# Loading chunk 4's queries after the second half of the values, behind a hold on chunk 2's third unit, in a fused sorted-attention and gated-MLP kernel

## The chip, the cores and the metric

The kernel runs on one core of one Trainium2 chip. The metric is the device time of one execution in microseconds (us), lower is better. The engines named below are TensorE (PE, matrix products and transposes by the identity), VectorE (DVE), ScalarE (ACT), GpSimd (POOL), and SyncE (SP), which here only issues DMAs. The DMAs of a core run on 16 DMA engines. Those that POOL issues stand in one queue (q0 in the profile, "software dynamic"), those that SP issues in another (q1, "hardware dynamic").

## What is computed

Two stages follow each other: attention over keys and values whose blocks are mixed by a normalized 8 x 8 matrix for each head, then a gated MLP with the cosine as gate. B = 4, H = 8, S = 768, D = 64, 8 blocks of 96 rows, 3072 tokens, model width 512, inner width 2048; inputs and output are float32.

```python
for _ in range(5):                       # P: (B, H, 8, 8), from sort_net
    P = exp(P - P.max(-1)); P /= P.sum(-1) + 1e-9; P /= P.sum(-2) + 1e-9
k_sorted = einsum('bhij,bhjcd->bhicd', P, k_blocks)
v_sorted = einsum('bhij,bhjcd->bhicd', P, v_blocks)
scores = q_blocks @ k_sorted_blocks.T / sqrt(D)      # 96 x 96 per block
attn = softmax(scores)
x = (attn @ v_sorted_blocks) -> (3072, 512)
h = x @ w_in
out = (h * cos(h)) @ w_out
```

## The kernel before

The 3072 tokens are worked on as eight chunks of 384 tokens, numbered 0 to 7: chunk n is one half (four blocks) of batch n // 2, for all 8 heads. A unit (n, u) is block u of chunk n, with its 8 heads. Batches 0 and 1 (chunks 0 to 3) are group 0, batches 2 and 3 (chunks 4 to 7) are group 1; keys and values of group 1 are loaded and sorted while chunks 1 to 3 are worked on.

The whole program is an order written out by hand (lines 845 to 1173): nothing reorders it, each engine runs its instructions in the order of the calls, and waits by semaphores where data or a buffer is not ready. The calls that matter here are:

- `qk(n, u)` (line 491; `qk_half` for one half): PE forms the scores of a unit (L438), DVE takes the row maximum (L487) and subtracts it (L489). `q_of(n, ...)` reads `q_turned[n % 2]`, so chunks 2, 4 and 6 share the tile `q_turned[0]`, and 3, 5 and 7 the tile `q_turned[1]`.
- `expo(n, u)` (line 510): ACT takes the exponential into one of three buffers `p_buf` (L515). With `on_pe` false SP then issues a DMA transpose of it into a tile called `pT` (L533), which is "the turn" of the unit; otherwise PE turns it later (`p_transpose`, L550).
- `av(n, u)` (line 555): PE multiplies the turned exponentials by the sorted values (L570), DVE divides by the sum (L581, L583). PE can't begin before the unit's turn has landed. Its PSUM tile comes from the pool `big`, which has three buffers that the scores, the key products (`k_sort_g`, L408, evicted by ACT) and others take in turn.
- `up`, `down`: the two products of the MLP (L614, L639); ACT takes the cosine (L618), DVE the gate (L622), and SP stores the result (L629).
- `load_q(n)` (line 115): from chunk 3 on, eight DMAs on POOL's queue (L129), one for each block and each parity of the head, which read 96 x 4 runs of 64 float32 numbers and write them as bf16. Chunks 4 and 6 go to the tile `q_mem`, chunks 3, 5 and 7 to a part of `kv` (the name of the tile that also holds the values).
- `q_transpose_dma(n)` (line 147): two DMA transposes on SP's queue (L149) which turn the loaded queries into `q_turned[n % 2]`. Each needs its half of the eight loads.
- `load_pair(vbuf, vin_d, lo, hi)` (line 90): one sixth of the values of group 1 on POOL's queue (L92). `v_permute` (line 169) are copies on POOL (L179) that put them into `vperm` in the order in which `v_sort_g` (L458) reads them.
- `p_hold(n, u)` (line 543): POOL copies one column of the unit's turn into a scrap tile `held` (L541). It computes nothing: it makes POOL wait until that turn has landed, and all that POOL issues later with it.
- `k_swap(kT2)` (line 420): two DMAs on SP's queue (L421, L422) that complete the sorted keys of group 1, which the scores of chunk 4 need.

POOL issues DMAs in eight lanes that are used in turn (semaphores DMASW0 to DMASW7): an issue waits until the DMA eight before it, on the same lane, has landed. SP's DMAs do the same with the lanes DMAHW0 to DMAHW7.

On POOL the stretch around the change stands in this order: `zeros_between(3)`, `load_q(3)`, a hold on keys, the first half of the values (three DMAs), `zeros_between(4)` (two memsets of `q_mem`, L137), `load_q(4)`, the hold on unit (2, 2), the second half of the values (three DMAs), `v_permute`, a memset, the hold on unit (3, 3), `load_q(5)`. On SP it is: `q_transpose_dma(3)`; the turns of units (2, 0), (2, 1), (2, 2); two stores; the turn of (3, 0); a store; `q_transpose_dma(4)`; `k_swap(kT2)`; the turns of (3, 1) and (3, 2). On PE, after the eight `up` of chunk 1 and scores of chunk 2, stand: parts of `down(1, ...)` with key products between, `av(2, 0)`, `qk(3, 0)`, key products, half of a `down`, key products, `av(2, 1)`, and so on.

Of the kernel before, what the change touches and what calls it, by code (L numbers as in the profile page):

```python
# [18 lines left out]
def kernel(  # L19
# [70 lines left out]
    def load_pair(buf, src, lo, hi):  # L90

        nc.gpsimd.dma_start(  # L92
            out=buf[:, lo:hi], in_=src[2:4].rearrange("b r x -> (b r) x")[:, lo:hi])
# [11 lines left out]
    def q_zeroed(n):  # L105

        return kbuf[:blk, :2 * (QZ + D)] if n % 2 else q_mem[:]
# [7 lines left out]
    def load_q(n):  # L115
        b, ih = n // 2, n % 2
        if n < NQ:

            nc.gpsimd.dma_start(
                out=q_rows, in_=q[b][:, ih * IC * blk:(ih + 1) * IC * blk].rearrange(  # L120
                    "h (p r) d -> p h (r d)", r=QR))
        else:
            src = q[b].rearrange("h (i c) d -> c i h d", c=blk).rearrange(
                "c i (h e) d -> c i h e d", e=2)
            q_heads = q_zeroed(n).rearrange("p (e x) -> p e x", e=2)[:, :, :QZ].rearrange(
                "p e (i h w) -> p i h e w", i=IC, h=H2)[:, :, :, :, :D]
            for i in range(IC):
                for e in range(2):
                    nc.gpsimd.dma_start(  # L129
                        out=q_heads[:, i, :, e], in_=src[:, ih * IC + i, :, e])  # L130
# [38 lines left out]
    def v_permute(rows, lo=0, halves=True, step=VQ, hi=D):  # L169

        for z in range(lo, hi, step):
            dst = vperm[rows, :CD].rearrange("p (d c) -> p d c", d=D)[:, z:z + step]
            src = vv[rows, z:z + step, :blk]
            if halves:
                dst = dst.rearrange("p d (x t) -> p d x t", x=2)
                src = src.rearrange("p d (t x) -> p d x t", x=2)
            nc.gpsimd.tensor_copy(dst, src)  # L179
# [231 lines left out]
    def k_sort_g(t0, eng, pool, tag):  # L411
        ps = pool.tile([128, 4, 4 * NB], FP32, name="ks", tag=tag)
        for t in range(4):
            k_products(ps, t, t0 + t, slice(0, 128), bds[1].rearrange("p x i -> p (x i)"),
                       pair)
        copy_on(
            eng, kT2[:, ::2, :, :, t0:t0 + 4].rearrange("p e b m t -> p b e m t"),
            ps.rearrange("p t (b e m) -> p b e m t", b=2, e=2))
# [91 lines left out]
    def expo(n, u, on_pe=False):  # L510
        p = p_bufs[cnt[0] % NP]
        cnt[0] += 1


        nc.scalar.activation(  # L515
            p[:, :, :blk], s_t.pop((n, u)).rearrange("p e h c -> p (e h) c"), AF.Exp,
            scale=scale)
        if u == 0 and n in (NQ, NQ + 1):

            w = 2 * H2 * blk  # L520
            c = 2 * (QZ + D) + (n - NQ) * w
            t = kbuf[:, c:c + w].rearrange("p (a c) -> p a c", c=blk)
        elif n < LATE:
            t = ptp.tile([128, 2 * H2, blk], BF16, name="pT", tag="pT")
        else:

            z, w = (n * IC + u) % 8, 2 * H2 * blk
            t = vperm[:, z * w:(z + 1) * w].rearrange("p (a c) -> p a c", c=blk)
        pT[n, u] = t
        if on_pe:  # L530
            pb[n, u] = p
        else:
            nc.sync.dma_start_transpose(out=t[:], in_=p.rearrange("p a c -> p (a c)"))  # L533
# [9 lines left out]
    def p_hold(n, u):  # L543
        hold(pT[n, u])
# [542 lines left out]
    expo(2, 3, True)  # L1087
    down(1, 1, 1, nc.sync)
    k_sort_g(12, A, *B)
    load_q(4)  # L1090
    p_hold(2, 2)
    for z in range(3, 6):
        load_pair(vbuf, vin_d, z * CD // 6, (z + 1) * CD // 6)
    expo(3, 0)
    v_permute(slice(0, 128))
    av(2, 1, True)
# [106 lines left out]
```

## Time and profile before

| | |
|---|---|
| Median of three runs | 239.36 us (236.26, 239.67, 239.36) |
| The profiled execution's own time | 238.81 us |
| Its span (first to last instruction) | 236.9 us |
| Outside of the span | 1.9 us |
| PE busy | 224.1 us, 95% of the span |
| DVE, ACT, POOL busy | 170.9, 154.6, 95.9 us |
| Mean granted PE clock over the span | 0.993 |
| DMA moved | 31.19 MB in 67672 packets |

All times within the span are counted from its start. A row of the timeline gives the start, the duration, the engine, the line, the operation, what it writes and reads, how many instructions are merged in it, and in brackets how long the engine sat idle before it and which instruction ended that. In the view by stretches "PEclk" is the clock that PE was granted, 1.00 being full, and "DMA share" is the summed busy time of packets over that of 16 engines. It can exceed 1, since the time of a packet counts from when it is begun, also while another is in work beside it.

### The profile page before, as it was taken

What the parts mean: (1) busy time and instruction counts of PE and PEld (TensorE: products, weight loads), DVE (VectorE), ACT (ScalarE), POOL (GpSimd) and SP (SyncE); (2) the same over time, 40 slices, a digit from 0 to 9 for tenths busy, and PEclk for the clock granted to TensorE, in tenths of its full rate; (3) what the DMA queues carried; (4) which work ended last, traced back from release to release, by engine and by line L of the source; (5) the groups of instructions that cost most, each with busy time, mean ns of one, the idle gap of its engine ahead of it and who ended that gap; (6) DMA issues with size and microseconds to landing.
All of it is one profiled execution on the core that took longest, in us unless ns stands there. A gap on an engine that the chain in (4) does not pass through costs nothing.

```text
span 236.9 us, 5401 instructions
## 1 busy us (share of the span) xinstructions
PE 224.1 (95%) x2191; PEld 142.1 (60%) x2212; DVE 170.9 (72%) x291; ACT 154.6 (65%) x209; POOL 95.9 (40%) x121
## 2 busy tenths in 40 slices
PE   8678999999999699999999999999999999999994
PEld 3367898567665366655666555655665566455554
DVE  6769867969699546895568985898599759835700
ACT  4648877777889347886788845673767466826611
POOL 8999998399992209900807100900000000000000
PEclk9999999999999799999999999999999999999999
DMA  7999999993999996659999778964942470251012
GB/s 91 209 196 205 204 221 217 201 237 100 112 151 157 175 190 128 68 133 162 106 155 115 79 92 148 220 67 92 165 161 38 81 199 0 50 157 46 3 44 89
DMA packets 67672, 31.19 MB, mean 132 GB/s; under 512 B 56384, under 2 KB 63168, under 8 KB 67392
## 3 DMA queue, kind: packets, MB, share of 16 engines
q0 software_dynamic: 24048, 13.64, 42.0%
q1 hardware_dynamic: 43312, 17.02, 34.7%
q8 instruction: 17, 0.28, 0.5%
q10 hardware_dynamic: 288, 0.20, 0.3%
q14 instruction: 7, 0.06, 0.1%
HBM read 27.27 MB, written 6.29 MB: 142 GB/s over the span
## 4 chain that ended last, share of the span: by engine, by line
PE 78%; DMA 10%; DVE 3%; POOL 3%; ACT 3%; issue 2%; SPq 0%; ACTq 0%; DVEq 0%; POOLq 0%
PE h L614 30%; PE o L639 24%; DMA kv<-in_v_dram 5%; PE h L798 5%; PE o L819 4%; DMA pT<-p_buf 4%; PE sc L438 4%; PE av L570 3%; POOL vperm L179 2%; PE o L1167 1%; DMA kTs<-kTs 1%; PE ks L408 1%; DVE xn L583 1%; PE vs L458 1%; ACT p_buf L515 1%
## 5 line engine op out<-in xcount | busy, mean ns | idle before, releaser
L614 PE MATMUL h<-xT,w_in_t 128*128 128x384 bf16 x448 | 78.4, 326 | 0.0
L639 PE MATMUL o<-w_out_t,gg 128*128 128x512 bf16 x305 | 75.2, 383 | 1.0 <-issue 0.2
L622 DVE TENSOR_TENSOR gg<-c,h 128x768 bf16<-128x768 f32 x56 | 52.7, 949 | 19.6 <-ACT c L618 19.6
L618 ACT ACTIVATE c<-h,half_pi 128x768 f32<-128x768 f32 x56 | 50.5, 901 | 24.6 <-PE h L614 23.6
L614 PEld LDWEIGHTS <-w_in_t 128*128 128x128 bf16 x448 | 42.2, 98 | 26.3 <-DVE xT L259 0.3
L639 PEld LDWEIGHTS <-gg 128*128 128x128 bf16 x320 | 29.5, 100 | 28.9 <-issue 1.7
L179 POOL COPY vperm<-kv 64x768 bf16<-64x768 bf16 (+2 forms) x12 | 28.3, 2398 | 10.2 <-PE xps L601 5.6
L515 ACT ACTIVATE p_buf<-s 96x768 bf16<-96x768 f32 x32 | 26.7, 843 | 5.5 <-DVE s L489 4.7
L489 DVE TENSOR_TENSOR s<-sc,mx 96x384 f32<-96x384 f32 (+1 forms) x33 | 24.3, 736 | 1.6
L487 DVE TENSOR_REDUCE mx<-sc 96x4 f32<-96x384 f32 (+1 forms) x33 | 24.0, 728 | 0.0
L583 DVE TENSOR_TENSOR xn<-av,r 96x512 bf16<-96x512 f32 x32 | 22.0, 686 | 1.1
L581 DVE RECIPROCAL r<-av 96x8 f32<-96x8 f32 x32 | 6.4, 199 | 15.2 <-PE av L570 15.0
L257 ACT CAST kTs<-ks 128x512 bf16<-128x512 f32 x20 | 11.3, 582 | 8.5 <-PE ks L408 7.5
L129 POOL DMA_DIRECT2D kv<-in_q_dram x24 | 16.0, 681 | 0.8 <-DMA xT<-xn 0.3
L438 PE MATMUL sc<-kTs,q_turned 128*128 128x96 bf16 x224 | 15.6, 207 | 0.4 <-DMA kTs<-kTs 0.4
L438 PEld LDWEIGHTS <-q_turned 128*128 128x128 bf16 x224 | 12.6, 98 | 4.1 <-DVE s L489 0.6
L257 ACT COPY kv<-o 128x512 f32<-128x512 f32 (+2 forms) x10 | 5.2, 524 | 14.1 <-PE o L639 11.5
L819 PE MATMUL o<-w_out_t,gg 128*128 128x512 bf16 x45 | 11.2, 379 | 0.2
L798 PE MATMUL h<-xT,w_in_t 128*128 128x192 bf16 x128 | 11.1, 246 | 0.0
L259 DVE COPY kv<-o 128x512 f32<-128x512 f32 (+1 forms) x5 | 3.1, 612 | 11.1 <-PE o L1167 8.5
L129 POOL DMA_DIRECT2D q_mem<-in_q_dram x16 | 10.7, 692 | 0.5 <-issue 0.5
L257 ACT COPY o_s<-o 128x512 f32<-128x512 f32 x8 | 4.7, 582 | 9.5 <-PE o L639 9.2
(128 smaller groups left out, 282.3 us busy)
## 6 DMA issues: line engine op xcount, KB each, us to landing
out_dram<-kv SPq DMA_DIRECT2D x12, 256.0 KB, 2.8
out_dram<-o_s SPq DMA_DIRECT2D x10, 256.0 KB, 3.2
w_in_t<-in_moe_w_in_dram POOLq DMA_DIRECT2D x4, 512.0 KB, 11.5
w_out_t<-in_moe_w_out_dram POOLq DMA_DIRECT2D x4, 512.0 KB, 12.4
kv<-in_k_dram POOLq DMA_DIRECT2D x2, 768.0 KB, 9.9
kv<-in_v_dram POOLq DMA_DIRECT2D x2, 768.0 KB, 13.3
pair<-in_k_dram POOLq DMA_DIRECT2D x2, 768.0 KB, 12.2
kv<-in_v_dram POOLq DMA_DIRECT2D x6, 256.0 KB, 5.3
```

The costliest lines, as they stand in the source:

```text
L129: nc.gpsimd.dma_start(out=q_heads[:, i, :, e], in_=src[:, ih * IC + i, :, e])
L179: nc.gpsimd.tensor_copy(dst, src)
L438: nc.tensor.matmul(out, q_of(n, hp)[:, x:x + 128], keys_of(n, u, h2, hp), start=True, stop=True)
L487: nc.vector.reduce_max(mx[:], scv, axis=AX.X)
L489: nc.vector.tensor_tensor(s, scv, mx.to_broadcast(list(s.shape)), op=ALU.subtract)
L515: nc.scalar.activation(p[:, :, :blk], s_t.pop((n, u)).rearrange("p e h c -> p (e h) c"), AF.Exp, scale=scale)
L583: nc.vector.tensor_tensor(xn.rearrange("p h e d -> p e h d"), avv[:, :, :, :D], r.to_broadcast([blk, 2, H2, D]), op=ALU.mult)
L614: nc.tensor.matmul(h[:, f2, :w], w_in_t[:, kk, f * 128:(f + 1) * 128], xT[n][:, kk], start=(kk == 0), stop=(kk == KC - 1))
L618: nc.scalar.activation(c[:], h[:, :, :w], AF.Sin, bias=half_pi[:, 0:1])
L622: nc.vector.tensor_tensor(gt[n, fp // 2][:, f:f + 2], c[:], h[:, :, :w], op=ALU.mult)
L639: nc.tensor.matmul(o[:], gt[n, f // 4][:, f % 4, ts * 128:(ts + 1) * 128], w_out_t[:, f, :], start=(f == 0), stop=(f == FC - 1))
L798: nc.tensor.matmul(o[:, part, f2 * w:(f2 + 1) * w], w_in_t[:, kk, f * 128:(f + 1) * 128], xT[0][:, kk, h * w:(h + 1) * w], start=(kk == 0) ...
```

## The change

One call is moved three statements down: `load_q(4)` stood ahead of the hold on unit (2, 2), and stands now behind that hold and behind the three loads of the values' second half.

```diff
     expo(2, 3, True)
     down(1, 1, 1, nc.sync)
     k_sort_g(12, A, *B)
-    load_q(4)
     p_hold(2, 2)
     for z in range(3, 6):
         load_pair(vbuf, vin_d, z * CD // 6, (z + 1) * CD // 6)
+    load_q(4)
     expo(3, 0)
     v_permute(slice(0, 128))
     av(2, 1, True)
```

The orders of PE, DVE, ACT and SP are as before; only POOL's differs. This is the place on POOL, with the memsets of `q_mem`, the eight loads of chunk 4's queries (L129), the hold (L541, `held`), the loads of the values (L92) and the copies of `v_permute` (L179); "x8" counts instructions that stand in a row:

```order
 L92 DMA kv<-in_v_dram 128x1024 x3
 L137 MEMSET q_mem 96x16x64 x2
-L129 DMA q_mem<-in_q_dram 96x4x64 x8
 L541 CAST held<-pT 96x1
 L92 DMA kv<-in_v_dram 128x1024 x3
+L129 DMA q_mem<-in_q_dram 96x4x64 x8
 L179 COPY vperm<-kv 128x1536 x4
 L227 MEMSET pair 96x128
```

The eight loads have moved past the hold and past the three loads of values, and stand directly ahead of the copies.

With the semaphores that each waits for, POOL's rows from the loads of the values on are these in the changed kernel (DMASW is a lane of POOL's DMAs):

```order
L92 DMA kv_87<-in_v_dram 128x1024 [waits DMASW4_49]
L92 DMA kv_87<-in_v_dram 128x1024 [waits DMASW5_49]
L92 DMA kv_87<-in_v_dram 128x1024 [waits DMASW6_49]
L129 DMA q_mem_93<-in_q_dram 96x4x64 [waits DMASW7_49]
...
L129 DMA q_mem_93<-in_q_dram 96x4x64 [waits DMASW4_49]
L129 DMA q_mem_93<-in_q_dram 96x4x64 [waits DMASW5_49]
L129 DMA q_mem_93<-in_q_dram 96x4x64 [waits DMASW6_49]
L179 COPY vperm_88<-kv_87 128x1536 [waits PE_49] x4
```

The last three loads of queries have taken the lanes 4, 5 and 6 behind the three loads of values, so each of them waits until one of these has landed; the copies no longer wait for these lanes themselves.

On SP the order is unchanged; only the lanes that the two transposes of chunk 4's queries wait for are others. The turn of unit (3, 0), a store, the two transposes and the two DMAs of `k_swap` stand so:

```order
 L533 DMA_TRANSPOSE kv<-p_buf_107 128x8x96 [waits DMAHW5_49,Activation_49]
 L629 DMA out_dram<-o_s 128x512 [waits DMAHW6_49,DVE_49]
-L149 DMA_TRANSPOSE q_turned_94<-q_mem 128x16x96 [waits DMASW4_49,DMASW2_49,DMASW6_49,DMASW0_49,DMAHW7_49,PE_49,Pool_49]
-L149 DMA_TRANSPOSE q_turned_94<-q_mem 128x16x96 [waits DMASW5_49,DMASW3_49,DMASW7_49,DMASW1_49,DMAHW0_49,PE_49,Pool_49]
+L149 DMA_TRANSPOSE q_turned_94<-q_mem 128x16x96 [waits DMASW5_49,DMASW3_49,DMASW7_49,DMASW1_49,DMAHW7_49,PE_49,Pool_49]
+L149 DMA_TRANSPOSE q_turned_94<-q_mem 128x16x96 [waits DMASW4_49,DMASW2_49,DMASW6_49,DMASW0_49,DMAHW0_49,PE_49,Pool_49]
 L421 DMA kTs<-kTs 64x3072 [waits DMAHW1_49,Activation_49]
 L422 DMA kTs<-kTs 64x3072 [waits DMAHW2_49]
```

Each transpose still waits for four of the eight loads, the last pair on the lanes 5 and 6 in the changed kernel, and what stands behind it in SP's queue has kept its place.

## The prediction

> **What bounds the kernel now.** I read the page first: which engine carries the chain that ended last, and where the clock that PE is granted falls. The third row has one digit for each fortieth of the span, 5.92 us.
>
> ```profile
> PE 224.1 (95%) x2191; PEld 142.1 (60%) x2212; DVE 170.9 (72%) x291; ACT 154.6 (65%) x209; POOL 95.9 (40%) x121
> PE 78%; DMA 10%; DVE 3%; POOL 3%; ACT 3%; issue 2%; SPq 0%; ACTq 0%; DVEq 0%; POOLq 0%
> PEclk9999999999999799999999999999999999999999
> ```
>
> PE is the bound: a saving must shorten PE's own time, or remove a wait of PE. The one digit under 9 lies at 77.0 to 82.9 us, just behind the change's place. So next I read PE's timeline there, PE in stretches of about 3.4 us, and the chain of waits.
>
> ```profile
> 77.30 0.39 PE L408 MATMUL ks<-bd,pair 128*128 128x128 bf16 x4
> 79.60 0.43 PE L570 MATMUL av<-vS,pT 96*128 96x65 bf16 x8 [1.92 <-DMA pT<-p_buf]
> 84.06 0.42 PE L570 MATMUL av<-vS,pT 96*128 96x65 bf16 x8
> 109.43 0.50 PE L438 MATMUL sc<-kTs,q_turned 128*128 128x96 bf16 x8
> ```
> ```profile
> 8.42:11.84 3.42, 2.07 (x36) 1.00 1.06 223
> 73.27:76.68 3.41, 3.38 (x29) 1.00 1.66 163
> 76.68:80.10 3.42, 1.50 (x22) 1.00 1.63 213
> 80.10:83.51 3.41, 3.19 (x17) 0.50 0.55 121
> ```
> ```profile
> 73.05 0.87 ACT p_buf L515 x2
> 73.92 5.64 DMA pT<-p_buf
> ```
>
> The columns of the second fence are the stretch, its length, PE's busy time and count, the granted clock, the DMA share and GB/s. PE stands still for 1.92 us from 77.68 to 79.60, because `av(2, 0)` needs the turn of unit (2, 0), which takes 5.64 us from its issue at 73.92. In the stretch that holds this wait PE is busy for 1.50 of 3.42 us; the stretch behind it runs at clock 0.50, the only such stretch between the start and the end. 2.07 busy us of 3.42, at 8.42, were enough to keep 1.00. So one late turn costs its wait and 3.41 us at half clock.
>
> Why is it late? The DMA queues say what else moved meanwhile: per queue the packets, MB and share of 16 engines, first for 65 to 71, then 71 to 73, then 72 to 78 us, and for comparison 144 to 148.5, where the same kind of transposes runs with no load on POOL's queue.
>
> ```profile
> q1 hardware_dynamic: 367, 0.09, 11.7%
> ```
> ```profile
> q1 hardware_dynamic: 962, 0.25, 105.6%
> ```
> ```profile
> q0 software_dynamic: 3022, 0.37, 99.8%
> q1 hardware_dynamic: 2289, 0.57, 73.5%
> ```
> ```profile
> q1 hardware_dynamic: 2994, 0.75, 92.2%
> ```
>
> From 72 to 78 POOL's queue has nearly all of chunk 4's queries in work: 8 loads of 96 x 4 runs are 3072 packets, and 3022 move there. SP's queue gets 2289 / 6 = 382 packets a microsecond beside them, against 2994 / 4.5 = 665 without. The timelines of POOL and SP give the order:
>
> ```profile
> 67.11 4.73 POOL L129 DMA_DIRECT2D q_mem<-in_q_dram  x7
> 81.06 0.18 POOL L541 CAST held<-pT 96x1 f32<-96x1 bf16 x1 [8.37 <-DMA pT<-p_buf]
> 81.53 1.63 POOL L92 DMA_DIRECT2D kv<-in_v_dram  x3 [0.29 <-issue]
> 88.80 11.26 POOL L179 COPY vperm<-kv 128x1536 bf16<-128x1536 bf16 x4 [5.64 <-PE xps L601]
> ```
> ```profile
> 65.19 8.01 SPq L149 DMA_TRANSPOSE q_turned<-kv  x2
> 73.92 4.94 SPq L533 DMA_TRANSPOSE pT<-p_buf  x3
> 91.32 3.70 SPq L149 DMA_TRANSPOSE q_turned<-q_mem  x2
> 100.92 0.47 SPq L421 DMA_DIRECT2D kTs<-kTs  x1
> 101.44 0.59 SPq L422 DMA_DIRECT2D kTs<-kTs  x1
> 105.59 1.22 SPq L533 DMA_TRANSPOSE pT<-p_buf  x1
> ```
>
> SP's queue holds chunk 3's two transposes of queries, then the three turns. Chunk 4's queries, issued from 67.11 on, are not needed before SP's two transposes at 91.32 and PE's scores of chunk 4 at 109.43.
>
> **The change, part by part.** Nothing is added or removed; eight loads on POOL pass a hold and three loads.
>
> First, the place they leave. The pair of transposes is 2 x 96 x 16 = 3072 packets of 256 B, a turn 768. By 71 us, 367 have moved, 2705 are left. At 665 a microsecond they end at 71 + 4.1 = 75.1, and the turn's 768 at 76.2. As the turn is issued at 73.92 and an unhindered one takes 2.9 us to land (the rows of issues below), it can't land before 76.8. At the slow end I take the 962 packets of 71 to 73, 481 a microsecond, while the loads had only begun: 71 + 5.6 + 1.6 = 78.2. PE is ready at 77.68. The wait of 1.92 becomes 0 to 0.5; I take 0.1, nearer to the quick end, because the row at 144 is the one without any load. Gain 1.8 us.
>
> With that wait gone PE is busy for over 2.8 of the 3.42 us, far above the 2.07 that kept the full clock, so the half clock should not come: 3.41 x 0.5 = 1.7 us. The Trainium skill (TensorE: Matmul & The Clock Gate, Part 1) puts the fall to half clock on about one idle window of 3.4 us and, under "Why this matters for your kernels", asks only for gaps under some 3 us. By that rule a gap of 1.92 us would not be the cause, removing it would not remove the slow stretch, and the sum would be -1.8. The trace differs from it: the two stand back to back at 1.92 us. The sum goes by the rows.
>
> What is late next? `av(2, 1)` takes the PSUM buffer of `qk(3, 0)`, which is free when DVE has subtracted the maximum:
>
> ```profile
> 81.96 0.95 DVE L489 TENSOR_TENSOR s<-sc,mx 96x768 f32<-96x768 f32 x1
> ```
>
> That ends at 82.91, 3.3 us behind the start of `av(2, 0)`. PE's work between the two `av` is 84.06 - 79.60 = 4.46 us, less 1.7 at full clock: 2.76. So a new wait of 3.3 - 2.8 = 0.5 us appears (0 to 0.6). The sum is -1.8 - 1.7 + 0.5 = -3.0 us. Behind it PE is dense (95% of the span) and all its feeders move with it, so I carry the 3.0 to the end.
>
> Second, POOL. The hold's wait was idle time and stays so. The turn of (2, 2), which ends it, lands earlier by some 1.5 us (its exponential on ACT is unchanged, so not by the whole gain), bounds 0 and 2.5. The values are then issued at 80.0 to 81.7 and land at 87.2, as they took until 88.80 from 81.53. Behind them come eight issues of 4.73 / 7 = 0.68 us, 5.4 in all. Five go out by 85.1, the last three wait on the lanes of the values and end at 87.9. Before, POOL only waited for the values in that time (5.64 us idle); the copies start at about 87.9, not at 88.80. Cover gone, it would be 5.4 us on copies that PE first reads at 104 us, 15 us after their start: cost 0.
>
> Third, the queries' arrival. In the order of the queue they move behind the values: 3072 packets at 3022 / 6 = 504 a microsecond from 87.2 on land at 93.3. SP's two transposes then start at 93.3, 2.0 us later than before, and occupy SP until 97.0. The next in its queue are the key swaps, in the new time 3.0 us earlier, at 97.9; the turn of (3, 1) comes at 102.6, chunk 4's scores at 106.4. All are met, by 0.9 us for the swaps' issue and more behind that. Cost 0, cover 0.9 us and 4 us of landing:
>
> ```profile
> vperm<-p_buf SPq DMA_TRANSPOSE x12, 2.9
> kTs<-kTs SPq DMA_DIRECT2D x2, 384.0 KB, 4.4
> ```
> ```profile
> DMA to landing us min/median/max: 2.4/5.4/14.3
> ```
>
> The sum against the profiled execution's own time is 238.81 - 3.0 = 235.8 us. That execution lies 0.55 us under the median of 239.36, so it is 3.6 us or 1.5% under the median, and inside the 2% (4.8 us) that is about what a measurement of this kernel can tell from no change.
>
> **Rivals.** *Hidden anyway.* The turn is late because of chunk 3's transposes and the values' first half, not of chunk 4's queries. For it: from 71 to 73 SP's queue moves only 481 a microsecond with few packets of queries beside it. Against: even at that rate the turn lands at 78.2. Were it to stay at 79.5, all stays: 238.8 us. Chance 0.12.
>
> *The half clock stays.* The wait shrinks but the slow stretch comes all the same, from what PE does around it, or because the remaining wait falls together with another. Against: the rows at 8.42 and 76.68 bracket the fall between 1.50 and 2.07 busy us. The time would be 238.8 - 1.8 = 237.0, the new wait being hidden by the slow clock. Chance 0.09. The rule of the Trainium skill above would give the same time.
>
> *Chunk 4 starves (slower).* The queries land so late that SP, which waits for them in order, holds back the key swaps and the turn of (3, 1). Its price starts when they land after 97.9 + 4.1 - 3.7 = 98.3: the swaps land 4.4 us behind their issue, and 106.4 - 97.9 - 4.4 = 4.1 us are to spare. From there each microsecond costs one; at 101.3 the gain is eaten, and 106.1 would be needed for 2% slower. The last query is issued at 87.9; with the longest landing of any load into this tile, 14.3 us, it lands at 102.2: 235.8 + 3.9 = 239.7, hardly slower. Only a POOL that issues far more slowly there would go further, and no row shows that. I give 0.09 to slower than before, of which 0.06 to more than 2%.
>
> *More than the sum.* The new wait of 0.5 does not come and later waits on turns shrink too (one of 0.38 us stands at 111.43 in PE's timeline, not counted above): from 235 down to 234. Chance 0.08.
>
> ```profile
> 111.43 0.43 PE L570 MATMUL av<-vS,pT 96*128 96x65 bf16 x8 [0.38 <-DMA pT<-p_buf]
> ```
>
> **How the numbers follow.** The forecast has 0.62, with an own range from 234.8 (238.8 - 1.9 - 1.7 - 0.4: no wait left, no new one, and the one at 111.43 gone too) to 236.9 (0.5 us more of the old wait left, and runs that lie 0.55 us over the profiled one, as the median of before does). The time is 235.8. The range goes from 234.2, within "more than the sum", up to 239.0, which takes in the half clock that stays and the hidden case; left out are the starving case and the lowest end, about 0.15. Faster by over 2% means under 234.6 against the median: 0.08 from "more", and 0.12 of the forecast, since the three runs of before alone lie 3.4 us apart: 0.20. Slower by over 2%: 0.06. Within: 0.74.
>
> **What would show it.** In the changed kernel's profile: no digit under 9 in PEclk near 80 us; the wait of `av(2, 0)` on its turn under 0.5 us, the turn landing within 4.3 us of its issue; SP's queue above 481 packets a microsecond from 72 to 76; the values issued near 80; the copies L179 starting by 89; SP's transposes from `q_mem` starting near 93 with the key swaps right behind the key products' eviction; the scores of chunk 4 near 106.4. Wrong would be: a wait of `av(2, 0)` near 1.9 us as before, a half clock without such a wait, or PE waiting for `q_turned` or `kTs` at chunk 4's first scores.

## The result, and the profile after

The changed kernel takes 235.09 us in the median of 20 runs (234.56 to 237.78), the kernel before 238.93 us in the median of 20 (236.26 to 241.02). The ratio of the times is 0.988, with a 95% interval from 0.985 to 0.992: a gain of about 1%, clear of noise and inside the 2%. The profiled execution took 235.54 us with a span of 233.6, so 3.27 us less than the profiled one of before.

The page's rows for PE, the chain that ended last, and the granted clock by fortieths of the span:

```profile
PE 224.1 (96%) x2212; PEld 141.8 (61%) x2212; DVE 171.0 (73%) x291; ACT 154.4 (66%) x209; POOL 95.9 (41%) x121
PE 82%; DMA 8%; DVE 3%; POOL 3%; ACT 1%; issue 1%; SPq 0%; ACTq 0%; DVEq 0%; POOLq 0%
PEclk9999999999999999999999999999999999999999
```

The dip of the clock is gone. PE's timeline at the place, and the same stretches of 3.4 us as before (length, PE's busy time and count, clock, DMA share, GB/s):

```profile
77.31 0.39 PE L408 MATMUL ks<-bd,pair 128*128 128x128 bf16 x4
77.53 0.42 PE L570 MATMUL av<-vS,pT 96*128 96x65 bf16 x8
78.37 0.38 PE L408 MATMUL ks<-bd,pair 128*128 128x128 bf16 x4
80.54 0.42 PE L570 MATMUL av<-vS,pT 96*128 96x65 bf16 x8
105.91 0.50 PE L438 MATMUL sc<-kTs,q_turned 128*128 128x96 bf16 x8
107.01 0.43 PE L570 MATMUL av<-vS,pT 96*128 96x65 bf16 x8 [0.60 <-DMA pT<-p_buf]
```
```profile
76.70:80.10 3.40, 3.33 (x35) 1.00 1.04 130
80.10:83.50 3.40, 3.40 (x48) 1.00 0.50 148
```

`av(2, 0)` starts at 77.53 where it started at 79.60 before, with no wait, and `av(2, 1)` at 80.54 where it started at 84.06: 2.07 us and then 1.45 us more are won, 3.52 in all. The DMA queues from 72 to 78 us say why. POOL's queue has nothing in that window, and SP's moves 3659 packets where it moved 2289:

```profile
q1 hardware_dynamic: 3659, 0.90, 73.9%
```

POOL and SP behind it:

```profile
81.23 0.18 POOL L541 CAST held<-pT 96x1 f32<-96x1 bf16 x1 [13.88 <-DMA pT<-p_buf]
81.68 1.60 POOL L92 DMA_DIRECT2D kv<-in_v_dram  x3 [0.27 <-issue]
83.23 4.06 POOL L129 DMA_DIRECT2D q_mem<-in_q_dram  x6
87.95 0.67 POOL L129 DMA_DIRECT2D q_mem<-in_q_dram  x1 [0.66 <-DMA kv<-in_v_dram]
92.22 0.67 POOL L129 DMA_DIRECT2D q_mem<-in_q_dram  x1 [3.59 <-DMA kv<-in_v_dram]
92.88 11.27 POOL L179 COPY vperm<-kv 128x1536 bf16<-128x1536 bf16 x4
```
```profile
73.93 3.88 SPq L533 DMA_TRANSPOSE pT<-p_buf  x3
82.35 1.22 SPq L533 DMA_TRANSPOSE kv<-p_buf  x1
94.42 3.58 SPq L149 DMA_TRANSPOSE q_turned<-q_mem  x2
98.09 1.13 SPq L421 DMA_DIRECT2D kTs<-kTs  x1
```

The hold ends at 81.23, no earlier than before (81.06). The last load of queries waits 3.59 us for the lane of the third load of values, and the copies start at 92.88, 4.1 us later than before. SP's two transposes of chunk 4's queries start at 94.42, 3.1 us later. Nothing of this reaches PE here: the scores of chunk 4 start at 105.91, 3.5 us earlier than before. Of the 3.52 us, 0.22 are lost to the turn of (3, 1), whose wait grew from 0.38 to 0.60 us; 3.27 remain at the end.

### The profile page after: what moved, and what is told of

Its sections match the earlier page's. It is cut to its first block, busy times and chain, and to the rows that moved or that the text cites. A ratio compares the mean times of both kernels' runs of the same rounds, so it can differ in the third digit from the quotient of the medians.

```text
span 233.6 us, 5420 instructions
## 1 busy us (share of the span) xinstructions
PE 224.1 (96%) x2212; PEld 141.8 (61%) x2212; DVE 171.0 (73%) x291; ACT 154.4 (66%) x209; POOL 95.9 (41%) x121
## 4 chain that ended last, share of the span: by engine, by line
PE 82%; DMA 8%; DVE 3%; POOL 3%; ACT 1%; issue 1%; SPq 0%; ACTq 0%; DVEq 0%; POOLq 0%
PE h L614 30%; PE o L639 27%; DMA kv<-in_v_dram 5%; PE h L798 5%; PE o L819 4%; PE sc L438 4%; PE av L570 3%; POOL vperm L179 3%; DMA pT<-p_buf 2%; PE ks L408 2%; PE o L1167 2%; DMA kTs<-kTs 1%; DVE xn L583 1%; PE vs L458 1%; PE pps L776 1%
## 5 line engine op out<-in xcount | busy, mean ns | idle before, releaser
L639 PE MATMUL o<-w_out_t,gg 128*128 128x512 bf16 x320 | 76.3, 379 | 0.0
L614 PEld LDWEIGHTS <-w_in_t 128*128 128x128 bf16 x448 | 42.2, 98 | 26.3 <-DVE xT L259 0.3
L179 POOL COPY vperm<-kv 64x768 bf16<-64x768 bf16 (+2 forms) x12 | 28.4, 2408 | 4.4 <-DMA kv<-in_v_dram 4.4
L129 POOL DMA_DIRECT2D kv<-in_q_dram x24 | 16.0, 677 | 0.8 <-issue 0.5
L129 POOL DMA_DIRECT2D q_mem<-in_q_dram x16 | 10.7, 690 | 4.6 <-DMA kv<-in_v_dram 4.2
L819 PE MATMUL o<-w_out_t,gg 128*128 128x512 bf16 x48 | 11.7, 379 | 0.0
L798 PEld LDWEIGHTS <-w_in_t 128*128 128x128 bf16 x128 | 10.5, 98 | 0.0
```

The lines of the kernel that those rows point to most:

```text
L129: nc.gpsimd.dma_start(out=q_heads[:, i, :, e], in_=src[:, ih * IC + i, :, e])
L614: nc.tensor.matmul(h[:, f2, :w], w_in_t[:, kk, f * 128:(f + 1) * 128], xT[n][:, kk], start=(kk == 0), stop=(kk == KC - 1))
L639: nc.tensor.matmul(o[:], gt[n, f // 4][:, f % 4, ts * 128:(ts + 1) * 128], w_out_t[:, f, :], start=(f == 0), stop=(f == FC - 1))
L798: nc.tensor.matmul(o[:, part, f2 * w:(f2 + 1) * w], w_in_t[:, kk, f * 128:(f + 1) * 128], xT[0][:, kk, h * w:(h + 1) * w], start=(kk == 0) ...
```

## The experiments

The theory: the eight loads share the 16 DMA engines with the turn of unit (2, 0) and delay it; PE waits; and the wait itself, by leaving PE idle, brings a stretch at half clock. Rivals: the turn is late for another reason; the slow stretch has another cause; the order against the values carries a part of the gain; the new place has a cost of its own. All times compare with executions of the kernel before on the same chip, taken beside them; "clock" is an execution's mean granted clock, where one stretch of 3.41 us at half clock in some 235 makes 0.993.

**The changed kernel again.**

> The changed kernel once more, as the base of the others. Theory (the query loads delay the turn of unit (2, 0), PE's wait for it brings the half clock): 3.0 to 3.5 us faster than before, 235 to 236 us, no wait of av(2, 0) over 0.5 us, no stretch at half clock near 80 us in its profile. Rival (the gain was the luck of one profile): within 1 us of before.

Measured: 235.65 us against 237.86 before, ratio 0.992 (0.988 to 0.996). The gain is no luck of one profile, but this profiled execution took 237.18 us at full clock, with a new wait at chunk 4's scores. Of this execution, first PE's timeline there, then SP's:

```profile
107.40 0.50 PE L438 MATMUL sc<-kTs,q_turned 128*128 128x96 bf16 x8 [1.05 <-ACT pair L257]
108.12 0.43 PE L570 MATMUL av<-vS,pT 96*128 96x65 bf16 x8 [0.22 <-DMA pT<-p_buf]
112.21 0.43 PE L570 MATMUL av<-vS,pT 96*128 96x65 bf16 x8 [0.36 <-DMA pT<-p_buf]
```
```profile
96.91 3.63 SPq L149 DMA_TRANSPOSE q_turned<-q_mem  x2
100.63 1.10 SPq L421 DMA_DIRECT2D kTs<-kTs  x1
101.79 0.59 SPq L422 DMA_DIRECT2D kTs<-kTs  x1
102.48 4.99 SPq L533 DMA_TRANSPOSE pT<-p_buf  x2
```

There is the starving rival, small: SP's transposes start 2.5 us later than in the first profile, SP issued the key swaps at 100.63, and the second landed at 107.26, just ahead of the scores at 107.40. (The row names ACT, but in the run "swap" below the same scores start ahead of the end of that ACT instruction.) It is 1.64 us over the first profile: 1.05 + 0.22 + 0.36 - 0.60 = 1.03 us are the waits here, and 0.28 were there already at `av(2, 0)`, which starts at 77.81 instead of 77.53.

**Waiting replaced by work.** The kernel before, with idle products on PE ahead of the late turn:

```diff
-    av(2, 0, True)
+    av_products(2, 0, fill=14)
+    av_norm(2, 0, True)
```

> The kernel before with 14 idle products of 256 columns (some 1.5 us) put ahead of av(2, 0) on PE: they fill the wait for the turn, and change nothing about it. Theory that idleness brings the half clock: the turn is still late, av(2, 0) still starts at 79.6, but no stretch at half clock follows; 1.7 us less than an execution of before that has the stretch, some 237. Rival, that the slow stretch has another cause: clock 0.50 near 80 to 83.5 stays and the time is that of before, 238.8 or more.

Measured: 237.82 us against 237.86, ratio 1.002 (0.998 to 1.005). In the profile no wait is left at that place and the clock stays full. PE's timeline shows the filler, and a wait further on:

```profile
77.68 1.72 PE L246 MATMUL av<-warm 128*128 128x256 bf16 x14
79.23 0.42 PE L570 MATMUL av<-vS,pT 96*128 96x65 bf16 x8
135.97 0.43 PE L570 MATMUL av<-pair,pT 96*128 96x65 bf16 x8 [1.15 <-DMA pT<-p_buf]
```

The clock went the way of the theory, on few executions: 3 of 12 at 0.993 or less, against 29 of 53 of the kernel before. The median did not: it is that of before. The profiled execution (237.53) was 0.5 us over the forecast, with a wait of 1.15 us for a turn of chunk 4 at 135.97, and the nine executions at full clock have a median of 237.53, 0.9 us over the full-clock ones of before (236.60). So what the filler saved in slow stretches it cost elsewhere. At the wait at 135.97 the loads of chunk 6's queries (issued from 126.71) ran beside the turns issued from 130.61: by the look of the timelines the same collision two chunks later; that was not tested.

**An idle PE without a DMA.** The changed kernel with a gap made by a hold and memsets on POOL; the argument `after` adds one small product that reads the zeros ahead of the unit's own:

```diff
-    zeros_between(4)
...
-    av(2, 0, True)
+    p_hold(2, 0)
+    nc.gpsimd.memset(q_mem[:, :QZ // 4], 0.0)
+    zeros_between(4)
+    av_products(2, 0, after=q_mem[:, QZ:QZ + D])
+    av_norm(2, 0, True)
```

> The changed kernel, with a wait of PE put in that no DMA has a part in: a hold on the turn of (2, 0), three memsets on POOL (2.4 us) behind it, and one small product that reads the last of them ahead of av(2, 0). PE stands still for some 2 us from 77.7, with the DMA queues as in the changed kernel. Theory, that PE's idleness and nothing else brings the half clock: in half of the runs or more a mean clock of 0.993 or less (the stretches stand at a place of their own in each run, and only one that holds most of the gap is short of work); full-clock runs at 236.8 to 237.2, the others 1 to 1.7 us over that. Rival, that the load on the DMA engines has a part in it: 0.993 no oftener than in the changed kernel (one run in four), and all runs near 237.

Measured: 237.63 us, ratio 1.001 (0.997 to 1.004): the gap alone gives the gain back. Its row in PE's timeline, and the stretch of 3.41 us that holds it with the one behind (counted from the trace's first clock record):

```profile
79.55 0.19 PE L566 MATMUL av<-q_mem,warm 96*128 96x64 bf16 x1 [1.72 <-POOL q_mem L137]
```
```profile
77.43:80.84 3.41, 1.64 (x28) 1.00 0.63 153
80.84:84.25 3.41, 3.41 (x33) 1.00 0.94 135
```

Six of 12 executions ran at full clock (0.998 and more), with a median of 236.78; six had at least one stretch at half clock, with a median of 238.39. The kernel before, over 53 executions on three chips (two of over 800 us left out): 24 at full clock, median 236.60; 20 with one stretch, 238.42; 9 with two or more, 239.69.

By the count alone, six of 12 against 10 of 38 of the changed kernel, this could be chance, since stretches elsewhere count too. The times say more. At 0.993 or less, and 1.3 us or more over their own kernel's full-clock median (a bound chosen afterwards), are 5 of 12 here and 22 of 53 of the kernel before, but 4 of 38 of the changed kernel and 1 of 46 of "fill", "noload", "swap", "swap2", "half" and "hold20". So 1.72 us of idleness without the query loads beside the turn does much what the late turn did: the rival of another cause falls. What decides in a single execution stays open. The profiled one ran at full clock, although the whole gap lies in one stretch; so the expectation's reason, that only the place of the stretches decides, does not hold here.

**The loads left out.** The kernel before without chunk 4's query loads (its queries are zeros):

```diff
-    zeros_between(4)
+    nc.gpsimd.memset(q_mem[:], 0.0)
...
-    load_q(4)
```

> The kernel before without the eight loads of chunk 4's queries; the memsets write all of q_mem instead, so chunk 4's queries are zeros: the loads are left out. Theory: the turn of (2, 0) lands by 77, no wait, no half clock, and the values' second half lands some 7 us after its issue, near 88.7; the time is that of the changed kernel, 235 to 235.5, because the loads cost nothing in their new place. Rival, that they still cost something there (the values' third load landed at 91.9 instead of 88.7): 0.5 to 1.5 us faster than the changed kernel. Rival, that the turn is late whatever the loads do: 238.8 as before.

Measured: 235.29 us, ratio 0.992 (0.988 to 0.995), beside 235.65 of the changed kernel on the same chip. The difference of 0.36 us, between 7 and 8 executions, is too small to tell from none. In the profile `av(2, 0)` does not wait, so the rival that the turn is late for another reason falls. The forecast of the values was wrong: with no queries behind them the copies still start late, in POOL's timeline of this run:

```profile
82.17 1.59 POOL L92 DMA_DIRECT2D kv<-in_v_dram  x3 [0.27 <-issue]
92.11 11.27 POOL L179 COPY vperm<-kv 128x1536 bf16<-128x1536 bf16 x4 [8.34 <-PE sc L438]
```

(The row names PE; in the run "late" below the same wait, 8.41 us, is put down to the DMA of the values.) So it isn't the queries behind the values that slow them.

**Half of the loads in the old place.**

```diff
+    load_q(4, 0, 2)      # blocks 0 and 1, the old place
     p_hold(2, 2)
     for z in range(3, 6):
         load_pair(vbuf, vin_d, z * CD // 6, (z + 1) * CD // 6)
+    load_q(4, 2, 4)      # blocks 2 and 3, the new place
```

> Four of the eight query loads stay in the old place, four go behind the values. Theory, that the packets of the loads share the DMA engines with the turns: half of the 3072 packets take about 3 us of the engines instead of 6, so the turn of (2, 0) lands between 76.9 and 79.5, near 77.5 to 78; the wait of av(2, 0) is under 0.7 us, no half clock; the time is 235 to 236. Rival, that any load issued in that place delays the turns by its start, not by its size: a wait near 1.9 us and the half clock, 238.8.

Measured: 235.09 us, ratio 0.989 (0.985 to 0.993), six executions from 234.49 to 235.31, all at full clock. The turn lands between the two cases, as sized: 4.06 us in the chain of waits, a wait of 0.34 us. The chain's row, and the queues from 72 to 78 us:

```profile
74.00 4.06 DMA pT<-p_buf
```
```profile
q1 hardware_dynamic: 3524, 0.88, 100.8%
q0 software_dynamic: 1577, 0.19, 53.1%
```

**No hold.** The values, too, are then issued at 67 us:

```diff
-    p_hold(2, 2)
     for z in range(3, 6):
         load_pair(vbuf, vin_d, z * CD // 6, (z + 1) * CD // 6)
     load_q(4)
```

> The changed kernel without the hold: values and queries are issued from 67 us on. Theory, that any traffic on POOL's queue from 70 to 79 us delays the turns: three loads of values (some 6 us of the engines) and the queries behind them; the turn of (2, 0) lands later than before, near 80 to 83, the wait of av(2, 0) is 2.5 to 5 us with the half clock behind it; 239 to 243. Rival, that the small packets of the queries alone do it and the values' large ones do not: as the changed kernel or 1 us slower.

Measured: 250.63 us, ratio 1.054 (1.049 to 1.059). The direction holds, the size doesn't: PE waits 13.60 us for the turn. PE's timeline, and the queues from 72 to 78 us:

```profile
91.49 0.65 PE L570 MATMUL av<-vS,pT 96*128 96x65 bf16 x8 [13.60 <-DMA pT<-p_buf]
```
```profile
q0 software_dynamic: 250, 0.37, 65.7%
q1 hardware_dynamic: 449, 0.11, 64.9%
```

From 72 to 78 us SP's queue moves 449 packets beside these 250, against 2289 in the kernel before beside 3022 packets of the queries, and both times POOL's queue moves 0.37 MB. So the loads of the values hold SP's queue up far more than the same amount of queries; that their larger packets are the reason was not tested. Behind so long a wait the mean clock falls to 0.973 or less in all four executions.

**The queries behind the copies.** The starving rival enforced:

```diff
-    load_q(4)
     expo(3, 0)
     v_permute(slice(0, 128))
+    load_q(4)
```

> The changed kernel with the queries issued behind the copies of the values too, so from about 100 us on: the starving rival, enforced. They land near 108; SP, which waits for them in order, issues the key swaps near 112 and they land near 116, where chunk 4's scores stood near 106. Theory (a microsecond lost for each behind 98.3 us): about 10 us slower than the changed kernel, 245, and up to 2 more if the half clock follows the wait. Rival, that chunk 4's queries have far more room than that: no slower than the changed kernel.

Measured: 251.09 us, ratio 1.056 (1.051 to 1.062), some 16 us over the changed kernel instead of 10 to 12. The timelines of SP and of PE:

```profile
109.77 3.61 SPq L149 DMA_TRANSPOSE q_turned<-q_mem  x2
113.47 1.16 SPq L421 DMA_DIRECT2D kTs<-kTs  x1
114.68 0.59 SPq L422 DMA_DIRECT2D kTs<-kTs  x1
```
```profile
120.18 0.80 PE L438 MATMUL sc<-kTs,q_turned 128*128 128x96 bf16 x8 [13.97 <-DMA kTs<-kTs]
```

The scores start 10.4 us behind the start of SP's transposes, not 8.1 (3.7 + 4.4). Of the 2.3 us, 1.1 were a slip: 4.4 is the median landing of the two swaps, and the scores need the second, which in the kernel before is issued 0.5 us behind the first and takes 5.0, so 5.5 from the first's issue. The rest is new: right behind the transposes the second is issued 1.2 us behind the first and takes 5.4, 6.6 in all. That the transposes' packets, ahead in the same queue, are the reason fits, but was not tested. "Again" shows the same distance, 107.40 - 96.91 = 10.5. PE's long wait also brings half clock, with a mean of 0.973 or less in all four executions, which the forecast put at up to 2 us; what it cost here was not measured.

**The hold on the first turn.** On POOL it stands at the same place:

```diff
+    p_hold(2, 0)
     av(2, 0, True)
...
-    p_hold(2, 2)
     for z in range(3, 6):
```

> The changed kernel with the hold on unit (2, 0) in place of (2, 2): POOL is let go when the first turn has landed, near 77, some 4 us earlier. Theory: values and queries land 3 to 4 us earlier (queries near 91, copies start near 89), the turns of (2, 1) and (2, 2) now share the engines with the values and land 1 to 2 us later; av(2, 1) at 80.5 waits 0 to 1 us; the time is that of the changed kernel within 0.7 us. Rival, that the late arrival of queries and values costs something in the changed kernel: 0.5 us or more faster. Rival, that the second turn becomes the next late one: 1 to 3 us slower.

Measured: 235.53 us, ratio 0.991 (0.988 to 0.995). That is the time of the changed kernel: the copies start at 88.70, and a wait of 0.64 us for the third turn appears at 83.89. The earlier values bought nothing that can be seen.

**The queries ahead of the values**, both behind the hold:

```diff
     p_hold(2, 2)
+    load_q(4)
     for z in range(3, 6):
         load_pair(vbuf, vin_d, z * CD // 6, (z + 1) * CD // 6)
-    load_q(4)
```

> The changed kernel with the queries ahead of the values, both behind the hold: only the passing of the hold remains of the change. Theory, that leaving the window from 67 to 79 us is the whole gain: the time of the changed kernel within 0.5 us; the queries land some 3 us earlier (near 91) and the values later (near 93 to 94), the copies start near 94. Rival, that the order against the values carries a part of the gain: 1 us or more slower than the changed kernel.

> The kernel with the queries ahead of the values once more, beside the changed kernel on the same chip. Theory, that in some runs of the changed kernel the queries arrive so late that SP holds back the key swaps and the turn of (3, 1), and that the order with the queries first frees it of that: 0.3 to 0.9 us faster than the changed kernel in the median, and no full-clock run over 236. Rival, that the two differ by chance: medians within 0.3 us, and the same tail.

> The changed kernel beside the run above. Theory: 235 to 235.8 us in the median, with some full-clock runs from 236 to 237.2. Rival: the same as the order with the queries first, within 0.3 us.

Measured: 234.78 and 234.89 us, ratios 0.991 (0.988 to 0.995) and 0.990 (0.985 to 0.995), beside 235.65 and 235.55 of the changed kernel on the same chips (the second with a ratio of 0.992, 0.988 to 0.996). So the order against the values carries no part of the gain: passing the hold is all of it.

Together the medians are 234.85 of 13 executions and 235.60 of 18; drawn again 20,000 times, their difference lies between -0.2 and -1.0 us in 95%. A part of it is the clock: 3 of the 13 ran at 0.993 or less, and 7 of the 18. Among the ten of each at full clock the medians are 234.79 and 235.24, and a difference of none is not ruled out (-1.0 to 0.0). In "swap" SP's transposes start at 88.76 and the swaps at 97.44, when the keys are ready, so the late swaps of "again" don't occur, though the copies start only at 96.15. That this makes the order faster was only argued; none of its full-clock executions is over 235.6, but in "again2" none was over 235.8 either, so the tail forecast for it did not show there.

## Why the prediction was right

**The turn and its wait.** The time was right, the rate by luck. From 71 us on SP's queue was sized at 665 packets a microsecond; it moved 2598 from 72 to 76, 650 a microsecond. But both are means over windows in which the queue also stands idle. SP's queue from 71 to 73 us, and what moved in each tenth of a microsecond from 72 to 76:

```profile
q1 hardware_dynamic: 1990, 0.50, 120.2%
```
```profile
GB/s 287 289 275 280 287 294 289 292 289 287 287 289 292 289 289 294 178 18 0 0 0 0 0 0 0 0 0 0 0 0 3 100 164 174 151 164 184 202 276 266
```

From 71 to 73 it moved 995 a microsecond, where the kernel before moved 481; chunk 3's transposes were done by 73.8, not at 75.1, and nothing moved until 75.0. The turn landed 3.0 us after its issue, near 76.9. So what set its time was the step named as a floor, an unhindered turn's 2.9 us from 73.92, and not the backlog that was added up. The predicted residue of 0.1 us was none. Over many executions the gain shows without the half clock's part in the full-clock medians, 236.60 us before and 235.07 of the changed kernel (24 and 27 executions): 1.5 us, for 1.8 less the small new waits.

**The half clock.** Right in cause, by "gap" and, on few executions, by "fill". Its price is 238.42 - 236.60 = 1.8 us, predicted 1.7. What the prediction missed is that it is a matter of chance in each execution: 29 of 53 at a clock of 0.993 or less before, 10 of 38 of the changed kernel. Stretches near the start, which the change does not touch, have a part in both counts. So the median moves by a share of it only, and the measured ratio says less than the two profiles. That the medians moved by 3.84 us, near the forecast 3.6, is partly luck: with 29 of 53 the median of before falls just among the slow executions. The bracket "1.50 brings it, 2.07 does not" was not sound: the stretch of "gap" with 1.64 busy us did not bring it, and in the profile of "swap2" one with 2.36 near the start did. That execution was only 0.4 us over the full-clock median of its order (235.19 against 234.79).

```profile
14.30:17.70 3.40, 2.36 (x52) 1.00 1.24 207
17.70:21.10 3.40, 3.40 (x73) 0.50 1.24 206
```

**The new wait of 0.5 us.** Near in size, wrong in cause. It is 3.01 us from `av(2, 0)` to `av(2, 1)` instead of 2.76, but the 0.24 us lie ahead of the key products at 78.37, which wait for ACT's eviction of the ones before. In the chain of waits of the changed kernel, and DVE's subtraction:

```profile
77.73 0.59 ACT kTs L257
78.37 0.38 PE ks L408 x4
```
```profile
79.89 0.95 DVE L489 TENSOR_TENSOR s<-sc,mx 96x768 f32<-96x768 f32 x1
```

The step "`av(2, 1)` takes the PSUM buffer of `qk(3, 0)`, which is free when DVE has subtracted the maximum" failed: `av(2, 1)` starts at 80.54 and the subtraction ends at 80.84, and in "half", "again" and "swap", too, the product starts first. That a wait of about the right size came from ACT is luck.

**POOL and the values.** Wrong, at no cost in the first profile. The step "the turn of (2, 2) lands earlier by some 1.5 us" failed: the hold ended at 81.23. In the packets, one engine's share of that turn ends at 80.3 where the others end by 78.9; it stands still while a packet of 16 KB that fetches instructions, begun at 78.83, takes 0.92 us. Two other profiles fit that: in "gap" this fetch comes only at 80.56, in "half" at 78.98 with the turn's last packet at 79.13, and there the hold ends at 79.68 and 79.83, near the 79.6 forecast. No run tested it. So the values did not move while PE and SP's turn of (3, 0), issued at 82.35 instead of 85.87, did. The step "land at 87.2, as they took" failed with it, by 4 to 5 us, and "noload" and "late" show that the queries are not the cause. That the turn of (3, 0) now runs among the values is what differs. The times line up with it: where that turn is issued 4.3 us behind the values, the copies start 7.3 us behind them (before); 2.4 us make it 8.3 ("half"), 0.7 and 0.6 us 9.9 and 10.0 ("noload", "late"). No run moved the turn alone.

**The queries' arrival.** The time was near (94.42 for 93.3), the cover not. "Its price starts when they land after 98.3" went by the median landing of the swaps, not the second's, and left out that they are slower right behind the transposes: the distance is 10.4 us, not 8.1, so with the scores at 105.91 they must be there by about 95.5. The first profile was within 1.1 us of that, and "again" over it. The starving rival, given 0.09 as a slower case, is part of the changed kernel's tail.

## What to carry to other kernels

Ask of each load not only when it is needed, but what stands in another queue on the same DMA engines while it moves: loads that were 20 us early delayed a transpose that PE was waiting for. A hold that lets go of a queue only after the urgent transfer costs nothing where that engine idles anyway, but what is behind it keeps its absolute time while the rest of the program moves up, so the slack has to be counted against the new times, with all that shares the queue. And a short idle time of TensorE can cost twice, once as a wait and, in some executions, once more as a slow clock.

## What was not expected of the hardware

In the profile of the kernel before, a gap of PE of 1.92 us was followed by a stretch of 3.41 us at half clock. In "gap", with 1.72 us, 5 of 12 executions had a low clock and were 1.3 us or more slower, which nearly doubles the price of the gap. Here the Trainium skill (TensorE: Matmul & The Clock Gate, "Why this matters for your kernels") asks only for gaps under some 3 us; the measurement decides. It does not come each time: 1.64 busy us in a stretch kept the full clock in one profile, and 2.36 lost it in another.

Beside 0.37 MB of values on POOL's queue (250 packets in 6 us) SP's queue moved 75 packets a microsecond, beside 0.37 MB of queries (3022 packets in 6 us) 382, and with POOL's queue all but empty 995 from 71 to 73 us.
